# A fused linear-attention and MLP kernel: a new order for every queue, the first chunk loads ahead of the weights, and eight PSUM banks in common

## The chip, the cores and the metric

The kernel runs on one core of a Trainium2 chip. The core has a matrix engine (PE), a vector engine (DVE), a scalar engine (ACT), a general engine (POOL) and a queue engine (SP) that issues its DMAs. Each engine takes its instructions in the order in which the program lists them, and waits for others by semaphores. The metric is the device time of one execution in microseconds.

## The reference

The first half is a gated linear attention, one state per batch and head. The second is an MLP with a hard-swish between its two matrix products.

```python
batch, n_heads, seq, head_dim = (4, 8, 768, 48)
...
for t in range(S):
    state = alpha[:, :, t, :, None] * state + np.einsum('bhd,bhe->bhde', k[:, :, t], v[:, :, t])
    y[:, :, t] = np.einsum('bhd,bhde->bhe', q[:, :, t], state)
...
x = np.ascontiguousarray(attn_out.transpose(0, 2, 1, 3)).reshape(B * S, H * D)
...
n_tokens, d_model, d_ff = (3072, 384, 2048)
h = x @ w_in
relu6 = np.clip(h + 3.0, 0.0, 6.0)
g = h * relu6 / 6.0
return (g @ w_out).astype(np.float32)
```

All arithmetic of the kernel is in 32-bit floats; the two MLP weights come in as 64-bit floats and are converted on the chip.

## The kernel before

**Tiling.** A chunk is 128 tokens of one batch: 24 chunks, six to a batch. Two chunks make a group of the MLP (256 tokens, 12 groups). The state is carried from chunk to chunk, with a half chunk (64 tokens) as the inner step.

**The order is written by hand.** The body is one list of 1788 words (lines 751 to 900) that `run` (line 745) takes one after the other; each word names a step, a chunk or group, and the buffers. `tc.manual_schedule()` keeps this order on every engine. So the word list gives, at one stroke, the order of PE, DVE, ACT, POOL and of SP's DMAs. A word of one engine that waits holds up the later words of that engine only.

**Words of the attention** (first number: the chunk). `la`, `lk`, `lq` (line 248) and `lv` (267) load alpha, k, q and v on SP. The first six chunks are loaded by token into `rings` (192 KB a load) and turned on PE by `ta`, `tk`, `tq` (274, L282); later ones come in blocks and are turned on DVE (L286), by `ca` for alpha. `ca` (297) places alpha: a copy on ACT (L300) for the first six. `r` (304, L309) and `p` (316, L320) are DVE scans that make the decays; `k` and `q` (324, L332) multiply by them on DVE. `kb` and `ck` (371, 376) turn k by token on PE and ACT; from chunk 8 on `kt`, `kw`, `kr` do it over DRAM. `sc` (338, L346) makes scores on PE, `m` (349, L356) masks them on DVE, `qa` (360, L366) and `sv` (412, L419) place q and the state with ACT. `u` (422, L429) is the state's update on PE, `sm` (434, L437 and L439) adds it on DVE, `st` (407, L409) decays the state on POOL. `ya`, `yb` (448, L455) make the output on PE, `cy` (461, L464) copies it to `xT` with ACT.

**Words of the weights** (16 slices of 768 KB: 0 to 7 of the first weight, 8 to 15 of the second). `w` (155, L162 and L166) loads a slice as pairs of 32-bit words. `d1` and `d2` (183, 194) take its low and high words on ACT, `dx` (188, L191) the sign on ACT for slices 0, 1, 2 and 4. `d3` (199) builds the bits on DVE: L207, L208 and L210, or L203 and L205 for the four. `d4` (213, L217) adds the low part on POOL. Five staging buffers (`raws`) are used in turn; two of them lie in the space of a later MLP result.

**Words of the MLP.** For the first two groups `f`, or `fa` and `fb` by halves (L478, L489), are the first product, `fr` and `fg` the gate on ACT and DVE, and `b` (L516) the second product of group 0. From group 2 on the first product is a fast matrix scheme with 20 products `M` (592, L600) in place of 24: `y` (577) makes 25 sums of weight blocks and `xc` (586) 11 sums of inputs on DVE (`add`, lines 537 to 541), `n` (604, L606) keeps partial results with ACT, `o` (608) makes outputs on DVE, `e` and `h` (619, 623) are the gate. The second product is a scheme of seven products `P` (685, L703) from group 1 on, with sums `x` of weights and `s` of hidden values (649, 658, L647), results kept by `K` (ACT) or put out by `G` (L719 on DVE, L716 on ACT), and `O` stores them. `z.m.n` (529, L532) issues n idle matmuls to bank m.

The two steps that the prediction speaks of most: `y.23` makes weight block 2 on DVE (L541), and `M.2.1`, the second product of group 2, is the first that reads it. `PRODUCTS` at line 560 pairs each product with its input and weight block.

**PSUM.** The attention's words name one of four banks `t0` to `t3` (`banks`, line 223), those of the MLP and the idle matmuls one of four banks `m0` to `m3` (`bank_m`, line 470). A step that starts a new result in a bank waits until the earlier result has been read out by ACT or DVE.

Of the kernel before, what the change touches and what calls it, by code (L numbers as in the profile page):

```python
# [17 lines left out]
def kernel(  # L18
# [42 lines left out]
    G = 2  # L61
# [161 lines left out]
    banks = [ps.tile([C, NP * C], FP, tag=f"t{i}", name=f"t{i}_ps") for i in range(4)]  # L223
# [246 lines left out]
    bank_m = [ps.tile([C, GT * 2], FP, tag=f"m{i}", name=f"m{i}_ps") for i in range(4)]  # L470

# [278 lines left out]
    with tc.manual_schedule():  # L750
        run("""z.0.5 z.0.3 z.0.1 z.0.8 qa.0.0 w.0 d2.0 d3.0 la.0 ta.0.0 ca.0 r.0 lk.0 tk.0.1 k.0
               z.0.2 p.0 la.1 ta.1.2 lq.0 tq.0.3 ca.1 r.1 lk.1 lv.0.0 sv.0.0 d1.0 kb.0.0 ck.0 z.0.2
               u.0.2.1 sm.0.0 sv.0.1 q.0 qa.0.1 tk.1.0 k.1 p.1 z.0.2 sc.0.2.3 m.0 la.2 ta.2.0 ca.2
               dx.0 w.2 d2.2 kb.1.0 ck.1 lq.1 r.2 sm.0.1 st.1 tq.1.2 q.1 d3.2 z.0.3 d1.2 dx.2 lv.1.1
               u.1.3.1 sv.1.0 sm.1.0 p.2 sm.1.1 sc.1.0.2 m.1 ya.0.3 yb.0 cy.0 lq.2 w.1 d1.1 tq.2.1
               q.2 d4.2 lk.2 tk.2.3 k.2 fa.2.0 d4.0 st.2 sc.2.0.2 d2.1 d3.1 m.2 dx.1 d4.1 qa.1.1
               lk.3 la.3 ta.3.1 ca.3 la.4 fa.0.1 sv.1.1 w.3 r.3 ta.4.3 ca.4 r.4 tk.3.1 k.3 kb.2.0
               qa.1.0 d2.3 ya.1.2 yb.1 cy.1 fa.1.2 lq.3 ck.2 d1.3 p.3 d3.3 lv.2.2 u.2.3.2 sm.2.0
               d4.3 fb.2 tq.3.1 q.3 fb.1 qa.2.0 sm.2.1 sv.2.0 st.3 fr.0.2.0 fg.0.2 lk.4 tk.4.0
               sv.2.1 w.5 d2.5 k.4 d3.5 d1.5 qa.3.0 d4.5 qa.2.1 sc.3.1.3 m.3 w.6 d2.6 d1.6 d3.6 d4.6  # L760
               lv.3.0 lq.4 w.7 kb.3.2 fb.0 f.0.3.3 kb.4.0 ya.2.1 ck.3 u.3.3.2 sm.3.0 fr.0.3.1 fg.0.3
               fr.0.1.0 fg.0.1 qa.3.1 sv.3.0 sm.3.1 p.4 d2.7 sv.3.1 d1.7 d3.7 d4.7 f.0.5.0 fr.0.5.1
               fr.0.0.0 fg.0.5 fg.0.0 tq.4.3 ck.4 la.5 ta.5.2 f.0.6.3 ca.5 w.4 d2.4 ya.3.0 yb.3 cy.3
               fr.0.6.1 yb.2 cy.2 w.9 d2.9 q.4 qa.4.1 d1.4 d1.9 dx.4 la.6 w.8 d3.4 r.5 lk.5 w.10
               d3.9 p.5 ca.6 fg.0.6 d4.9 w.12 lq.5 lv.4.1 d2.8 d3.8 f.0.7.2 d1.8 st.4 d4.8 d4.4 w.11
               fr.0.7.0 fg.0.7 f.1.7.0 fr.1.7.1 fg.1.7 sc.4.0.2 m.4 f.1.1.1 fr.1.1.0 fg.1.1 f.1.3.3
               fr.1.3.1 d2.10 d1.10 tk.5.3 f.1.0.2 d2.12 d3.10 d4.10 w.13 fg.1.3 fr.1.0.0 fg.1.0 k.5
               d3.12 lq.6 f.1.6.0 f.1.2.1 u.4.1.0 sm.4.0 d1.12 d4.12 sv.4.0 qa.4.0 ya.4.2 fr.1.6.1
               fg.1.6 w.15 tq.5.3 fa.4.3 sv.4.1 d2.11 kb.5.1 d2.13 fr.1.2.0 f.1.4.2 fr.1.4.1 d1.11
               sm.4.1 q.5 r.6 d3.11 d3.13 fg.1.4 d4.11 lv.5.0 lk.6 tq.6 p.6 d2.15 d3.15 fg.1.2 d1.13  # L770
               d4.13 sc.5.0.3 yb.4 f.1.5.0 fr.1.5.1 fg.1.5 tk.6 m.5 b.1.0.2 fb.4 b.1.1 d1.15 d4.15
               st.5 y.5 w.14 la.7 lk.7 cy.4 d2.14 qa.5.1 ck.5 b.0.0.1 fr.0.4.0 d3.14 k.6 q.6 ca.7
               fg.0.4 d1.14 d4.14 x.0 y.1 y.10 b.0.1 y.0 y.2 u.5.2 P.1.0.0 K.1.0 qa.5.0 sv.5.0
               qa.6.1 P.1.1.3 b.0.2 b.1.2 kb.6.0 ya.5.3 y.6 s.1.0.0 sm.5.0 sv.5.1 G.1.0.0 tk.7
               s.1.1.1 s.1.2.3 x.1 yb.5 cy.5 b.1.3 sc.6.1.2 lv.6.2 ck.6 u.6.3.0 s.1.3.2 x.2 P.1.2
               b.0.3 K.1.1 y.7 s.1.4 s.1.5 y.11 y.3 r.7 xc.2.1 x.3 y.4 y.8 xc.2.3 k.7 xc.2.0 xc.2.4
               y.9 y.12 y.16 y.13 y.15 P.1.3.3 K.1.2 P.1.4 bo.1 P.1.5 xc.2.5 G.1.1.1 P.1.6 y.14 y.17
               y.19 xc.2.6 sm.6.0 G.1.2.2 y.20 M.2.0.2 lv.12.1 la.8 O.1.1 O.1.0 ca.8 y.18 y.21 y.23
               so.1 G.1.3.3 n.2.0.8 bo.0 lq.7 lv.7.0 O.1.2 m.6 xc.2.2 xc.2.10 xc.2.7 tq.7 r.8 p.7
               xc.2.8 sv.6.1 M.2.15.3 M.2.1 kb.7.3 n.2.1.9 M.2.16 M.2.2 n.2.2.10 M.2.7.0 n.2.7.11  # L780
               sm.6.1 xc.2.9 q.7 p.8 M.2.3 M.2.4 n.2.4.12 M.2.8 o.2.0.0 M.2.5 n.2.5.13 qa.7.0 sv.6.0
               st.7 lk.8 O.1.3 lq.8 lk.9 la.9 la.10 tk.8 tq.8 lq.10 lq.9 ya.6.1 yb.6 M.2.9 z.1.3
               M.2.18.1 o.2.1.0 e.2.1.1 M.2.10 cy.6 ck.7 sc.7.0.2 u.7.1.3 n.2.10.14 M.2.11 qa.7.1
               ca.9 la.11 y.22 M.2.6.2 h.2.1 q.8 m.7 e.2.0.0 h.2.0 n.2.11.15 qa.6.0 n.2.18.10 qa.8.1
               M.2.12 M.2.19 n.2.12.12 M.2.13 sm.7.0 sv.7.1 r.9 k.8 o.2.3.0 sv.7.0 ya.7.0 y.24
               o.2.5.0 n.2.13.12 o.2.2.0 yb.7 cy.7 sc.8.1.2 xc.3.1 o.2.2.1 e.2.2.1 xc.3.3 o.2.3.1
               M.2.14 xc.3.4 xc.3.0 xc.3.5 o.2.4.0 xc.3.7 xc.3.6 o.2.6.0 P.2.0.1 M.3.0.2 M.2.17
               h.2.2 o.2.6.1 e.2.3.0 h.2.3 o.2.7.0 K.2.0 n.3.0.12 M.3.1 n.3.1.9 e.2.5.1 M.3.7.0
               n.3.7.13 xc.3.8 o.2.7.1 xc.3.2 kt.8 e.2.6.0 h.2.6 tk.9 M.3.2 n.3.2.10 e.2.4.0 P.2.1.3
               h.2.4 h.2.5 s.2.0.14 e.2.7.0 G.2.0.1 h.2.7 M.3.3 M.3.4 n.3.4.8 k.9 s.2.1.11 M.3.8  # L790
               o.3.0.0 ca.10 kt.9 P.2.3.3 s.2.2.15 s.2.3.14 lv.8.2 kw.8 kr.8 lk.10 sm.7.1 xc.3.9
               M.3.5 n.3.5.11 K.2.2 e.3.0.1 xc.3.10 M.3.9 o.3.1.0 P.2.2 K.2.1 u.8.0.3 M.3.18.2 s.2.5
               M.3.10 n.3.10.14 n.3.18.15 e.3.1.0 s.2.4 P.2.4 tq.9 h.3.0 st.8 sv.8.0 M.3.11 n.3.11.8
               tk.10 p.9 sm.8.0 q.9 r.10 k.10 qa.9.0 qa.9.1 m.8 sm.8.1 h.3.1 M.3.19 o.3.5.0 kt.10
               P.2.5 G.2.2.0 st.9 M.3.12 sc.9.0.1 qa.8.0 n.3.12.10 o.3.3.0 kw.9 lv.9.0 kr.9 sv.8.1
               u.9.2.3 sm.9.0 sv.9.1 sv.9.0 G.2.1.2 sm.9.1 st.10 M.3.15.2 M.3.16 M.3.6.3 M.3.13 m.9
               o.3.4.0 o.3.6.0 tq.10 n.3.13.10 o.3.2.0 e.3.4.1 ya.8.2 yb.8 ya.9.3 yb.9 cy.9 M.3.14
# [135 lines left out]
```

## Time and profile before

| | |
|---|---|
| median of three runs | 535.38 us (535.36 to 535.48) |
| span of the profiled execution, first to last instruction | 533.7 us |
| PE busy | 524.6 us, 98% |
| DVE busy | 477.2 us, 89% |
| ACT busy | 257.2 us, 48% |
| POOL busy | 50.4 us, 9% |
| DMA queue of the program | 53.44 MB, 42.5% of the 16 engines' time |
| first transposes of loaded data on PE (L282) | at 8.05 us |
| last copy, on ACT (L716) | 530.86 to 531.18 us |

The profiled execution has no total of its own beside the span; the runs' median is 1.7 us above it. PE here is the matmul row; a 32-bit matmul takes several passes and shows as two instructions (58 for the 29 idle matmuls), a transpose as one. Durations of neighbouring instructions of one engine overlap a little: a DVE step of 0.68 us that follows another without a wait starts 0.60 us after it.

### The profile page before, as it was taken

What the parts mean: (1) busy time and instruction counts of PE and PEld (TensorE: products, weight loads), DVE (VectorE), ACT (ScalarE), POOL (GpSimd) and SP (SyncE); (2) the same over time, 40 slices, a digit from 0 to 9 for tenths busy, and PEclk for the clock granted to TensorE, in tenths of its full rate; (3) what the DMA queues carried; (4) which work ended last, traced back from release to release, by engine and by line L of the source; (5) the groups of instructions that cost most, each with busy time, mean ns of one, the idle gap of its engine ahead of it and who ended that gap; (6) DMA issues with size and microseconds to landing.
All of it is one profiled execution on the core that took longest, in us unless ns stands there. A gap on an engine that the chain in (4) does not pass through costs nothing.

```text
span 533.7 us, 15143 instructions
## 1 busy us (share of the span) xinstructions
PE 524.6 (98%) x6306; PEld 499.4 (94%) x6306; DVE 477.2 (89%) x849; ACT 257.2 (48%) x503; POOL 50.4 (9%) x71
## 2 busy tenths in 40 slices
PE   8799999999999999999999999999999999999997
PEld 7698886789999999999999999999999999999997
DVE  6999989999999999998999999999999899496382
ACT  3889865212653553553544444642634544553340
POOL 5333425100000000000000000000000000000000
DMA  9998876005615155254344355044454042100001
GB/s 174 217 252 256 215 216 152 21 2 154 152 30 116 32 121 135 57 140 95 87 110 113 91 124 140 19 120 102 115 136 104 11 110 43 44 2 2 15 16 37
DMA packets 124100, 54.40 MB, mean 102 GB/s; under 512 B 83328, under 2 KB 116864, under 8 KB 124032
## 3 DMA queue, kind: packets, MB, share of 16 engines
q1 hardware_dynamic: 124032, 53.44, 42.5%
q8 instruction: 49, 0.80, 0.6%
q14 instruction: 19, 0.16, 0.1%
HBM read 44.50 MB, written 8.91 MB: 100 GB/s over the span
## 4 chain that ended last, share of the span: by engine, by line
PE 85%; DVE 8%; POOL 2%; DMA 2%; ACT 1%; issue 1%; SPq 1%; DVEq 0%; POOLq 0%
PE m_ps L703 34%; PE m_ps L600 34%; PE m_ps L478 5%; PE t_ps L455 4%; PE t_ps L346 2%; PE t_ps L429 2%; PE m_ps L489 2%; PE t_ps L282 1%; DVE rings L647 1%; DMA v<-in_v_dram 1%; DVE raw L537 1%; ACT raw L191 1%; DMA kq<-in_k_dram 1%; DVE g_sb L647 1%; DVE w L537 1%
## 5 line engine op out<-in xcount | busy, mean ns | idle before, releaser
L606 ACT COPY g_sb<-m_ps 128x512 f32<-128x512 f32 x110 | 63.6, 584 | 124.9 <-PE m_ps L600 104.1
L703 PE MATMUL m_ps<-w,g_sb 128*128 128x192 f32 x704 | 121.7, 327 | 0.0
L703 PEld LDWEIGHTS m_ps<-w,g_sb 128*128 128x128 f32 x704 | 113.7, 190 | 0.4
L703 PE MATMUL m_ps<-rings,g_sb 128*128 128x192 f32 x528 | 91.5, 326 | 0.0
L703 PEld LDWEIGHTS m_ps<-rings,g_sb 128*128 128x128 f32 x528 | 85.4, 190 | 0.1
L600 PE MATMUL m_ps<-xc,w 128*128 128x128 f32 x640 | 82.7, 277 | 0.3 <-DVE w L541 0.3
L600 PEld LDWEIGHTS m_ps<-xc,w 128*128 128x128 f32 x640 | 77.5, 192 | 1.5 <-issue 0.5
L494 ACT ACTIVATE r<-g_sb,half 128x512 f32<-128x512 f32 x80 | 56.8, 722 | 32.9 <-DVE g_sb L541 12.1
L498 DVE SCALAR_TENSOR_TENSOR g_sb<-r,g_sb 128x512 f32<-128x512 f32 x80 | 53.6, 682 | 4.6 <-ACT r L494 4.2
L600 PE MATMUL m_ps<-xT,raw 128*128 128x128 f32 x400 | 52.5, 277 | 0.0
L600 PEld LDWEIGHTS m_ps<-xT,raw 128*128 128x128 f32 x400 | 48.6, 192 | 0.6
L409 POOL TENSOR_TENSOR st<-sm,R 128x192 f32<-128x192 f32 x20 | 12.9, 643 | 353.8 <-DVE sm L439 306.7
L647 DVE TENSOR_TENSOR g_sb<-g_sb 128x512 f32<-128x512 f32 (+1 forms) x55 | 42.0, 795 | 0.2
L600 PE MATMUL m_ps<-xT,w 128*128 128x128 f32 x320 | 42.0, 276 | 0.0
L600 PEld LDWEIGHTS m_ps<-xT,w 128*128 128x128 f32 x320 | 39.3, 192 | 0.1
L366 ACT COPY A<-q 48x256 f32<-48x256 f32 x88 | 35.5, 404 | 5.0 <-DVE q L332 3.7
L356 DVE TENSOR_TENSOR A<-t_ps,mask 64x256 f32<-64x256 f32 x96 | 36.0, 414 | 0.4
L478 PE MATMUL m_ps<-xT,w 128*128 128x256 f32 x144 | 32.8, 382 | 0.0
L600 PE MATMUL m_ps<-xc,raw 128*128 128x128 f32 x240 | 31.8, 276 | 0.0
L309 DVE TENSOR_TENSOR_SCAN R<-t,ones 128x516 f32<-128x516 f32 x24 | 29.7, 1236 | 1.1 <-ACT t L300 1.0
L478 PEld LDWEIGHTS m_ps<-xT,w 128*128 128x128 f32 x144 | 26.7, 190 | 3.6
L600 PEld LDWEIGHTS m_ps<-xc,raw 128*128 128x128 f32 x240 | 29.6, 192 | 0.1
(104 smaller groups left out, 731.0 us busy)
## 6 DMA issues: line engine op xcount, KB each, us to landing
raw<-in_moe_w_out_dram SPq DMA_DIRECT2D x8, 768.0 KB, 5.2
raw<-in_moe_w_in_dram SPq DMA_DIRECT2D x6, 768.0 KB, 6.8
v<-in_v_dram SPq DMA_DIRECT2D x48, 96.0 KB, 3.0
out_dram<-oh SPq DMA_DIRECT2D x44, 96.0 KB, 1.7
far<-kq SPq DMA_DIRECT2D x64, 64.0 KB, 2.2
kb<-far SPq DMA_DIRECT2D x64, 64.0 KB, 2.0
aq<-in_alpha_dram SPq DMA_DIRECT2D x36, 96.0 KB, 2.5
qq<-in_q_dram SPq DMA_DIRECT2D x36, 96.0 KB, 2.4
```

What stands on the lines that cost most here:

```text
L309: nc.vector.tensor_tensor_scan(out=reverse(R, n - 1, n), data0=reverse(ax, n, n), data1=reverse(ones, n, n), initial=0.0, op0=ALU.mult, op ...
L356: nc.vector.tensor_tensor(out=to[:, a], in0=sc[a][half], in1=mask[half, half].unsqueeze(1).to_broadcast([HB, NP, HB]), op=ALU.mult)
L366: nc.scalar.copy(out=to[:, a], in_=Q_t[j][64 * a : 64 * a + D, :, half])
L409: nc.gpsimd.tensor_tensor(out=st, in0=sm, in1=R_t[j][:, :, 0:1].to_broadcast([C, NP, D]), op=ALU.mult)
L455: nc.tensor.matmul(y_of(j, (i + 1) // 2, p)[:, HB * b : HB * b + HB], vb[:, p, e : e + 32], A_t[j][:, b, 2 * p + a], start=(b == 0 and i = ...
L478: nc.tensor.matmul(h[:, f], w1[:, kk, o : o + C], xT_t[g][:, kk], start=(kk == 0), stop=(kk == KT - 1))
L494: nc.scalar.activation(out=to, in_=h, func=AF.Relu, bias=half, scale=1.0 / 6.0)
L498: nc.vector.scalar_tensor_tensor(out=to, in0=r, scalar=1.0, in1=h, op0=ALU.min, op1=ALU.mult)
L600: nc.tensor.matmul(acc[g][i][:, f * C : (f + 1) * C], spots[w][:, f * C : (f + 1) * C], x_of(g, x), start=(first and f == 0), stop=last, s ...
L606: nc.scalar.copy(out=slots[z], in_=acc[g][i])
L647: nc.vector.tensor_tensor(out=out, in0=in0, in1=in1, op=ALU.subtract)
L703: nc.tensor.matmul(to[g], a, rhs[:, f], start=(first and f == 0), stop=(last and f == HF - 1), skip_group_check=True)
```

## The change

One line exchanges the bank lists, so that both halves of the kernel can name all eight banks (for the attention, 4 to 7 are the MLP's, and the other way round), and the whole word list is replaced. The steps are the same 1788, the same 29 idle matmuls among them; their order and their buffers differ. At the head of the list ten loads of chunks 0 to 2 and weight slice 1 now come ahead of slice 0, which was the first transfer; only five idle matmuls stand in front of the first transposes, against seventeen; and five idle steps (ten matmuls) stand in the middle of the first third. Around the first products of group 2 some attention steps of chunks 7 to 9 have moved ahead of `y.23`.

```diff
     bank_m = [ps.tile([C, GT * 2], FP, tag=f"m{i}", name=f"m{i}_ps") for i in range(4)]
+    banks, bank_m = banks + bank_m, bank_m + banks
...
-        run("""z.0.5 z.0.3 z.0.1 z.0.8 qa.0.0 w.0 d2.0 d3.0 la.0 ta.0.0 ca.0 r.0 lk.0 tk.0.1 k.0
-               z.0.2 p.0 la.1 ta.1.2 lq.0 tq.0.3 ca.1 r.1 lk.1 lv.0.0 sv.0.0 d1.0 kb.0.0 ck.0 z.0.2
-               u.0.2.1 sm.0.0 sv.0.1 q.0 qa.0.1 tk.1.0 k.1 p.1 z.0.2 sc.0.2.3 m.0 la.2 ta.2.0 ca.2
-               dx.0 w.2 d2.2 kb.1.0 ck.1 lq.1 r.2 sm.0.1 st.1 tq.1.2 q.1 d3.2 z.0.3 d1.2 dx.2 lv.1.1
...
-               d4.13 sc.5.0.3 yb.4 f.1.5.0 fr.1.5.1 fg.1.5 tk.6 m.5 b.1.0.2 fb.4 b.1.1 d1.15 d4.15
-               st.5 y.5 w.14 la.7 lk.7 cy.4 d2.14 qa.5.1 ck.5 b.0.0.1 fr.0.4.0 d3.14 k.6 q.6 ca.7
...
-               y.19 xc.2.6 sm.6.0 G.1.2.2 y.20 M.2.0.2 lv.12.1 la.8 O.1.1 O.1.0 ca.8 y.18 y.21 y.23
-               so.1 G.1.3.3 n.2.0.8 bo.0 lq.7 lv.7.0 O.1.2 m.6 xc.2.2 xc.2.10 xc.2.7 tq.7 r.8 p.7
-               xc.2.8 sv.6.1 M.2.15.3 M.2.1 kb.7.3 n.2.1.9 M.2.16 M.2.2 n.2.2.10 M.2.7.0 n.2.7.11
...
+        run("""z.2.5 la.0 ta.0.0 z.7.3 qa.0.0 ca.0 lk.0 tk.0.0 la.1 z.0.3 ta.1.6 ca.1 lq.0 lk.1 r.0
+               k.0 p.0 kb.0.4 ck.0 r.1 tq.0.7 lv.0.0 sv.0.0 tk.1.0 lq.1 k.1 u.0.1.2 q.0 qa.0.1 la.2
+               kb.1.5 sm.0.0 sm.0.1 st.1 w.1 ck.1 sv.0.1 p.1 tq.1.6 sc.0.1.0 lv.1.1 sv.1.0 lk.2 q.1
+               qa.1.0 ta.2.5 ca.2 m.0 sc.1.2.7 w.0 d1.1 m.1 d2.1 d3.1 z.0.8 dx.1 lq.2 qa.1.1
...
+               fg.0.6 lq.5 r.5 tq.5.3 q.4 w.7 p.5 w.4 kb.4.5 d1.7 lk.6 ck.4 lv.4.1 sv.4.0 w.9 d2.7
...
+               d4.8 b.1.0.4 d3.10 la.6 ca.6 w.11 fr.1.0.0 d4.3 fg.1.0 fg.1.1 d1.10 f.1.3.3 z.6.3
+               d1.11 sv.4.1 lq.6 fr.0.4.0 f.1.2.0 d4.10 d3.12 w.13 qa.4.1 z.2.1 tk.6 r.6 k.6 d1.12
...
+               z.4.2 bo.0 y.10 s.1.4 G.1.0.1 y.8 z.6.2 y.2 y.0 y.4 lq.9 y.12 y.16 q.7 xc.2.0 xc.2.7
+               s.1.5 qa.7.1 K.1.1 P.1.4 y.14 y.9 y.15 y.13 y.17 y.19 K.1.2 P.1.5 O.1.0 G.1.1.1
+               O.1.1 xc.2.8 y.20 x.3 sc.6.7.0 lk.9 kb.7.3 y.18 G.1.2.0 tq.8 qa.7.0 O.1.2 M.2.0.5
+               st.7 n.2.0.8 P.1.6 lv.7.2 y.21 y.23 la.10 M.2.1 m.6 M.2.7.1 n.2.1.15 M.2.2 xc.2.9
...
```

## The prediction

> **What bounds the kernel now.** I read the page's shares first, then the table of stretches, then the waits of PE, then the timeline at the places these point to.
>
> ```profile
> PE 524.6 (98%) x6306; PEld 499.4 (94%) x6306; DVE 477.2 (89%) x849; ACT 257.2 (48%) x503; POOL 50.4 (9%) x71
> ...
> 24.00:76.00 52.00, 51.52 (x682) 45.42 (x681) 49.66 (x82) 45.45 (x76) 21.54 (x19) 1.00 0.89 233
> 76.00:128.00 52.00, 51.75 (x438) 41.12 (x436) 51.40 (x77) 15.45 (x32) 8.89 (x14) 1.00 0.34 79
> 128.00:424.00 296.00, 295.96 (x3809) 291.04 (x3810) 284.09 (x520) 141.99 (x297) 10.12 (x15) 1.00 0.43 100
> ```
>
> The columns after the length are PE, PEld, DVE, ACT, POOL. From 128 us on PE is busy 295.96 of 296 us, and the waits of PE after 128 us are one of 0.3 us. So behind that point nothing can be gained: time is saved only by getting PE to this point earlier, or by having less PE work left there. From 76 to 128 us DVE is just as full (51.40 of 52). The place where the two meet:
>
> ```profile
> 127.20 0.69 DVE L541 SCALAR_TENSOR_TENSOR w<-w 128x512 f32<-128x512 f32 x1
> ...
> 128.04 1.13 PE L600 MATMUL m_ps<-xc,w 128*128 128x128 f32 x8 [0.29 <-DVE w L541]
> ```
>
> The first line is step `y.23`, the second is `M.2.1`, which waits for it. Hence the frame of my sum: **span = time at which DVE ends `y.23` + PE work from `M.2.1` on + tail.** Now that is 127.9, then from 128.04 to PE's end at 530.84, then 2.9 us for the last copy and store: 533.7. The runs' median is 535.38, 1.7 above the span; I carry this 1.7 unchanged.
>
> How DVE got to 127.9:
>
> ```profile
> 8.05 1.04 PE L282 MATMUL t_ps<-ident,rings 128*128 128x128 f32 x8
> ...
> 9.31 1.23 DVE L309 TENSOR_TENSOR_SCAN R<-t,ones 128x516 f32<-128x516 f32 x1 [1.02 <-ACT t L300]
> ...
> 72.56 0.36 DVE L439 TENSOR_TENSOR s<-t_ps,st 128x192 f32<-128x192 f32 x1 [1.28 <-PE t_ps L429]
> ...
> 82.47 1.78 DVE L207 TENSOR_SCALAR w<-w 128x768 f32<-128x768 f32 x1
> ...
> 92.80 1.95 DVE L332 TENSOR_TENSOR q<-q,P 128x512 f32<-128x512 f32 x1
> ```
>
> From the first scan (`r.0`, 9.31) DVE runs 118.6 us to the end of `y.23`. Its steps up to there, each at the time from its start to the next one's start (0.60 for a 128x512 of 0.68, since neighbours overlap by 0.08: the pair of L498 takes 1.28), make 110.6. The rest, 8.0, is the one wait of 1.28 at 72.56; 3.4 in four steps that stretch while POOL runs an add (L207 1.78 where it takes 0.55 elsewhere, `q.6` 1.95 where it takes 0.69, and two smaller ones at 26.1 and 29.4); and 3.2 in small pieces.
>
> **The change part by part.**
>
> *The PE list as work.* Both lists hold the same 1788 steps, the idle matmuls (29, 58 instructions) included. PE's work is the same; only places differ. From `M.2.1` to the end, counted with 0.112 us a pass of L600, 0.163 of L703 and 0.48 of a `ya` or `yb`, the old list has 398.6 us left and the new one 398.4: **-0.2**. (The actual 402.8 from 128.04 to 530.84 has 4.2 more, about 0.1 at each change of kind; no wait, so I keep it.)
>
> *The DVE list.* Every DVE step that stands before `y.23` in the old list also stands before it in the new one. Nine more do: `ca.9`, `tq.7`, `tq.8` (three L286 transposes, 0.95 each), `p.7` (1.14), `q.7` (0.66), `sm.6.1` (0.27) and three `xc` (0.20 each), taken from the same rows: 2.85 + 1.14 + 0.66 + 0.27 + 0.60 = **+5.5**. They are in front of `M.2.1` on a full engine, and `M.2.1` is in front of everything else on PE. They are not lost work (less is left for later), but later DVE has time to spare, as it idles 107 - 73 = 34 us from 424 on, so it buys nothing at the end. The same holds a little behind: before `o.2.1.0` there are 6.5 us more, so moving the meeting point does not mend it.
>
> *First loads in front of the weights.* On SP `w.0` (768 KB, ahead of all) goes behind ten chunk loads and `w.1`. ACT starts on `w.0` at 5.63, so that load took 4.9 us from its issue at 0.75; a store of 192 KB lands in 2.0 us in the table of issues. `la.0` is 192 KB and first now: between these ends, 3.5, so it lands at 4.3. The way from the first transposes to the scan (8.05 to 9.31) is 1.26; these four now run at the first matmuls' rate, 0.2 us apart instead of 0.11 (34 idle ones in 6.75 us against 4 in 0.61 later): 0.4 more. `r.0` at about 6.15, so DVE is 3.2 earlier. But `d3.0`, two instructions of 1.39 us, ran in the hole in front of `r.0` and now stands behind it on the full engine. Net **-1.8**, bounds -2.5 (the five idle matmuls that stay in front hold PE to 3.7) and -0.4 (4.9 us for the load).
>
> *Waits on the way.* The 1.28 at `sm.4.0` came from PE being late with `u.4`; in the old list PE has 59.6 us of steps up to `u.4` and DVE 60.1 ahead of `sm.4.0`, in the new one 45.6 and 47.2, so PE is more ahead there: **-1.3** (bounds -1.3 and 0). Against that `r.1` and `k.1` follow transposes on a PE that is still at the slow rate, with `z.7.3` and `z.0.3` between them, and `d3.5` comes a microsecond earlier on DVE while its `w.5` has 22 loads in front of it instead of 21: I put **+0.5** (bounds 0 and 2: the row for it is the 2.39 us for which DVE waited on `w.0`).
>
> *Row first, then a page:* the old list's 34 idle matmuls keep PE busy from 1.46, and the spacing drops from 0.213 to 0.111 us at 7 us. The Trainium skill, "TensorE: Matmul & The Clock Gate", Part 1, has the clock at half by default, released by about 3.4 us of sustained activity. The new list has 5 idle matmuls ahead of `ta.0` and then a hole; by that rule full speed could come a window later, and about 1.5 us would be added to the start, by the row alone 0.5.
>
> *POOL's adds.* 16 (L217, 1.5 to 1.9 us each) lie before `y.23` in both lists. The rows show that a DVE step which reads SBUF alone (L207, L309, `q.6`) is held when it starts under an add, while L498, L356 and L439, which read PSUM, are not. I keep **3.4** for the new list, change 0 (bounds -3.4, no step held, and +3.4, twice as many: `d4.1`, `d4.8`, `d4.13` and `d4.14` are followed by SBUF steps in the new list).
>
> *Eight shared banks.* PE's waits that can be a bank not yet drained stand before 30 us (L374 on ACT's L300 0.7, L282 on DVE's L439 0.3 and L356 0.2); no DVE step waited for PE until 72.56, so they are not on the path. What the sharing allows by itself is worth **0** (bounds -0.3, the one wait from 128 us on, and +0.5 for a bank that now waits for the slower of two uses, as those first waits of 0.2 to 0.7).
>
> *SP, ACT.* The same transfers and copies; behind 50 us the DMA engines are under half busy, ACT is at 48%. Nothing added. ACT is full only from 24 to 76 us (45.45 of 52), where conversions come later by one load; that is in the 0.5.
>
> *Sum:* +5.5 - 0.2 - 1.8 - 1.3 + 0.5 = **+2.7**: `M.2.1` at about 131, span 536.4, time 535.38 + 2.7 = 538.1.
>
> **The rivals.**
>
> 1. *POOL's adds miss DVE (the other side).* If the new list puts a PSUM-reading step under each add, the 3.4 us go; then +2.7 - 3.4 = -0.7: 534.7. From 0.7 us of stretch on (0.3 with `r.0` half a microsecond earlier as well, 534.2) the new kernel is ahead. For it: behind `d3.5`, `d3.9` and `d3.10` stand 2 us of PSUM steps. Against: behind `d3.8` comes `d3.3`, behind `d3.14` come `q.6` and the `y` steps, all from SBUF.
> 2. *Weights too late.* Eight chunk loads in front of `w.1`, and `la.5`, `lk.5`, `lq.5` in front of `w.7`: DVE waits for `d3.5`, `d3.6` or `d3.7` while the DMA engines are saturated (0.89 of their time from 24 to 76 us). At 2.2 us for one weight load a wait of one to two loads: +2.7 + 2.2 to 4.4 = 540.3 to 542.5. Against: by the order of loads only `w.5` comes within a microsecond of its use.
> 3. *It does nothing.* DVE is not the bound up to `y.23`, since PE waited only 0.29 us for it, and PE's early work, equal in both, decides. Then the earlier start and the later `d3.0` cancel to within 1 us: 534.5 to 536.4. Against: a step that is 5.5 us late on a full engine is not hidden by a slack of 0.29.
>
> **How the numbers follow.** The forecast, with its terms near the middle (536.5 to 540), has 0.54; rival 2 0.12; rival 3 0.16; rival 1 0.18, of which two thirds lie below 534.3. About 0.2% (1.07 us) is what a measurement of this kernel can tell from no change. Faster by more than that: rival 1's lower part, 0.13. Within: the rest of rival 1 and rival 3, 0.21. Slower: 0.66. All bounds on the good side add up to -2.2 (533.2), all on the bad side to +10.8 (546.2); with 2 in 10 left out, 533.8 to 541.8.
>
> **What would show it.** Right: `r.0` starts near 6.2; the DVE step before `M.2.1` ends near 131, with PE idle for microseconds between 90 and 135 us, where it now idles 0.3; PE's waits after `M.2.10` are small again; the tail is 2.9. Wrong: `r.0` after 7, the start is mis-sized; `M.2.1` before 128, then DVE's stretch, in particular under L217, was smaller; PE waits after 150 us, then DVE stayed the bound beyond the meeting point and the loss is larger; a wait of DVE for ACT at L203 or L207 between 20 and 50 us is rival 2.

## The result and the profile after

The changed kernel takes **560.66 us** (median of four runs, 557.9 to 561.81) against 535.43 for the one before: a ratio of 1.0463, 95% interval 1.0436 to 1.049. The forecast was 538.1, range 533.8 to 541.8: the sign was right, the size was wrong by 22.6 us.

The profiled execution of after has a span of 559.6 us, 26.0 more than before. The share of PE on its page, then its table of the same three stretches (length, then PE, PEld, DVE, ACT, POOL, granted clock, DMA share, GB/s):

```profile
PE 534.1 (95%) x6306; PEld 504.6 (90%) x6306; DVE 490.9 (88%) x849; ACT 257.6 (46%) x503; POOL 50.0 (9%) x71
```

```profile
24.00:76.00 52.00, 47.05 (x594) 40.79 (x592) 48.91 (x75) 38.16 (x61) 18.46 (x23) 0.97 0.97 234
76.00:128.00 52.00, 47.86 (x374) 37.42 (x374) 51.23 (x71) 20.42 (x38) 11.17 (x9) 1.00 0.38 103
128.00:424.00 296.00, 288.20 (x3695) 280.57 (x3696) 281.60 (x508) 133.98 (x280) 8.45 (x14) 0.99 0.41 94
```

PE idles 5.0, 4.1 and 7.8 us in the three stretches, where it idled 0.5, 0.3 and 0.04. DVE is as full as it was. The clock, 1.00 throughout before, is 0.97 and 0.99 in two rows: the records of after show three stretches of 3.4 us at half rate, at 25.5, 131.3 and 343.0 us.

The timeline of after at the start and at the meeting point (start, length, engine, line, operation; in brackets the idle time before it and what ended it):

```profile
5.87 1.23 DVE L309 TENSOR_TENSOR_SCAN R<-t,ones 128x516 f32<-128x516 f32 x1 [1.69 <-ACT t L300]
...
139.41 2.77 PE L704 MATMUL m_ps<-rings,g_sb 128*128 128x192 f32 x16
...
140.24 0.69 DVE L542 SCALAR_TENSOR_TENSOR w<-w 128x512 f32<-128x512 f32 x1
...
142.02 1.05 PE L601 MATMUL t_ps<-xc,w 128*128 128x128 f32 x8
```

`r.0` starts at 5.87 (before 9.31). `y.23`, the DVE line, ends at 140.9 (before 127.9). `M.2.1`, the last line, starts at 142.02 (before 128.04); it comes 1.1 behind `y.23`, because `P.1.6` in front of it was itself late, behind a PE that had stood still and then run at half rate. From `M.2.1` to PE's end at 556.80 pass 414.8 us (before 402.8), and the tail is 2.8. So the 26.0 are **14.0 ahead of `M.2.1` and 12.0 behind it**. Behind it PE waits again; the waits of PE in after from there on (line, what it waited for, us in total, times, longest):

```profile
PE t_ps L429 <- DMA kb<-far: 1.4, 2, 0.8
PE t_ps L601 <- DVE g_sb L540: 1.1, 1, 1.1
PE m_ps L429 <- DMA kb<-far: 0.9, 2, 0.7
...
PE t_ps L601 <- ACT g_sb L607: 0.5, 1, 0.5
```

They come to 5.5 us, the last of more than half a microsecond at 364; the same view of before has 0.3 in all, the wait in front of `M.2.1` itself. But the waits are only half of the 12.0. PE's stretch from `M.2.1` to its end, before and then after (length, then PE, PEld, DVE, ACT, POOL, granted clock, DMA share, GB/s):

```profile
128.04:530.82 402.78, 402.78 (x4906) 396.46 (x4906) 357.04 (x656) 182.07 (x377) 11.15 (x17) 1.00 0.35 83
```

```profile
142.02:556.80 414.78, 408.72 (x4905) 399.37 (x4904) 356.77 (x645) 180.98 (x372) 9.77 (x16) 1.00 0.32 75
```

After's PE stands still for 6.1 us of it; for the other 5.9 it is shown busy longer with the same work. The half-rate stretch at 343.0 makes at most 1.7 of these; what the remaining 4.2 are, no view names. The chain of waits of after also goes through DVE far behind the meeting point. This is its order of time (start, length, engine and line):

```profile
183.78 1.02 DVE R L309
...
184.93 0.66 DVE k L332
185.59 0.61 DVE g_sb L538
...
186.24 1.17 PE t_ps L601 x8
...
187.44 0.69 DVE g_sb L542
188.13 0.62 DVE kq L391
```

A scan and a scaling of a later chunk's attention (L309, L332) stand ahead of a sum of the MLP (L538) for which PE waits, here 0.28 us; then the chain is on DVE again. What PE waits for is not an input: the sum reads out the bank that PE's next product writes. A late DVE holds PE in this way too, by a bank that is not yet free.

**Theory A**, formed on this: in the new list PE and DVE stay level up to about 365 us, so whatever holds DVE is paid, also behind `M.2.1`; in the old list DVE runs ahead from 128 us on. **Theory B**: the 12.0 belong to the new rest's own order, banks or transfers. **Theory C**: all of it comes from the head.

### The profile page after: what moved, and what is told of

Read it like the earlier page. It is cut to its first block, busy times and chain, and to the rows that moved or that the text cites. A ratio compares the mean times of both kernels' runs of the same rounds, so it can differ in the third digit from the quotient of the medians.

```text
span 559.6 us, 15091 instructions
## 1 busy us (share of the span) xinstructions
PE 534.1 (95%) x6306; PEld 504.6 (90%) x6306; DVE 490.9 (88%) x849; ACT 257.6 (46%) x503; POOL 50.0 (9%) x71
## 4 chain that ended last, share of the span: by engine, by line
PE 49%; DVE 33%; issue 5%; DMA 4%; ACT 4%; SPq 4%; POOL 1%; DVEq 0%; POOLq 0%; ACTq 0%
PE m_ps L704 16%; PE t_ps L601 15%; PE m_ps L601 6%; PE t_ps L704 6%; DVE g_sb L499 3%; DVE g_sb L538 3%; DVE R L309 3%; DMA aq<-in_alpha_dram 2%; DVE P L320 2%; DVE g_sb L648 2%; DVE k L286 1%; DVE A L356 1%; DVE q L286 1%; DVE k L332 1%; SPq L404 1%
## 5 line engine op out<-in xcount | busy, mean ns | idle before, releaser
L607 ACT COPY g_sb<-t_ps 128x512 f32<-128x512 f32 x74 | 43.0, 584 | 89.7 <-PE t_ps L601 81.1
L704 PE MATMUL m_ps<-w,g_sb 128*128 128x192 f32 x432 | 75.4, 327 | 1.3 <-DVE g_sb L665 1.3
L704 PEld LDWEIGHTS m_ps<-w,g_sb 128*128 128x128 f32 x432 | 70.3, 191 | 2.6 <-DVE g_sb L665 1.6
L601 PE MATMUL t_ps<-xc,w 128*128 128x128 f32 x384 | 51.3, 278 | 2.7 <-DVE g_sb L540 1.1
L601 PEld LDWEIGHTS t_ps<-xc,w 128*128 128x128 f32 x384 | 47.1, 191 | 4.2 <-DVE g_sb L540 1.3
L704 PE MATMUL t_ps<-w,g_sb 128*128 128x192 f32 x272 | 47.2, 327 | 0.0
L704 PEld LDWEIGHTS t_ps<-w,g_sb 128*128 128x128 f32 x272 | 43.9, 190 | 0.1
L607 ACT COPY g_sb<-m_ps 128x512 f32<-128x512 f32 x36 | 20.9, 584 | 35.6 <-PE m_ps L601 28.1
L538 DVE TENSOR_TENSOR g_sb<-g_sb 128x512 f32<-128x512 f32 x40 | 27.0, 684 | 10.8 <-ACT g_sb L607 10.4
L601 PE MATMUL m_ps<-xc,w 128*128 128x128 f32 x256 | 33.7, 276 | 0.0
L309 DVE TENSOR_TENSOR_SCAN R<-t,ones 128x516 f32<-128x516 f32 x24 | 30.9, 1286 | 1.8 <-ACT t L300 1.7
L601 PEld LDWEIGHTS m_ps<-xc,w 128*128 128x128 f32 x256 | 31.2, 192 | 0.2
```

The source lines that it names most:

```text
L309: nc.vector.tensor_tensor_scan(out=reverse(R, n - 1, n), data0=reverse(ax, n, n), data1=reverse(ones, n, n), initial=0.0, op0=ALU.mult, op ...
L538: eng.tensor_tensor(out=out, in0=in0, in1=in1, op=ALU.add if s1 > 0 else ALU.subtract)
L601: nc.tensor.matmul(acc[g][i][:, f * C : (f + 1) * C], spots[w][:, f * C : (f + 1) * C], x_of(g, x), start=(first and f == 0), stop=last, s ...
L607: nc.scalar.copy(out=slots[z], in_=acc[g][i])
L704: nc.tensor.matmul(to[g], a, rhs[:, f], start=(first and f == 0), stop=(last and f == HF - 1), skip_group_check=True)
```

## The experiments

All times beside 535.4 to 535.7 us for the kernel before on the same chip. "Rest" is PE's time from `M.2.1` to its end. The median is of all executions of a run; `y.23`, `M.2.1`, rest and span are of the one that was profiled, and executions of one kernel with the new list or a part of it differ by 2 to 4.4 us. Kernels with "small adds" or "short h" leave out part of the arithmetic.

| run | median us | ratio, 95% interval | `y.23` ends | `M.2.1` | rest | span |
|---|---|---|---|---|---|---|
| before | 535.4 | | 127.9 | 128.0 | 402.8 | 533.7 |
| after | 560.7 | 1.0463 (1.0436 to 1.049) | 140.9 | 142.0 | 414.8 | 559.6 |
| e1, old head, new rest | 559.9 | 1.0459 (1.0426 to 1.0492) | 127.8 | 128.0 | 425.7 | 556.4 |
| e7, the same, loads mended | 558.7 | 1.0430 (1.0415 to 1.0445) | 127.7 | 127.9 | 425.1 | 555.8 |
| e2, new head, old rest | 550.7 | 1.0278 (1.0258 to 1.0298) | 140.5 | 142.6 | 403.0 | 549.6 |
| e3, new, small adds | 552.3 | 1.0314 (1.0289 to 1.0339) | 133.6 | 133.8 | 412.5 | 549.1 |
| e4, old, small adds | 534.8 | 0.9988 (0.9979 to 0.9998) | 127.2 | 127.3 | 402.8 | 533.0 |
| e5, new, short h | 553.0 | 1.0330 (1.0315 to 1.0345) | 142.8 | 142.9 | 407.2 | 553.0 |
| e6, old, short h | 535.4 | 0.9997 (0.9988 to 1.0006) | 127.9 | 128.0 | 402.8 | 533.6 |
| e9, new, both | 548.1 | 1.0230 (1.0215 to 1.0246) | 135.3 | 135.4 | 406.4 | 544.7 |
| e10, new, nine behind | 560.5 | 1.0465 (1.0449 to 1.0481) | 135.6 | 136.2 | 420.6 | 559.6 |
| e8, old, loads first | 535.1 | 0.9999 (0.9986 to 1.0012) | 127.1 | 127.2 | 402.8 | 532.9 |
| e11, old, faster start | 536.9 | 1.0024 (1.0013 to 1.0035) | 131.8 | 132.0 | 402.8 | 537.6 |
| e12, old, warm start | 534.7 | 0.9982 (0.9974 to 0.9991) | 127.2 | 127.3 | 402.8 | 532.9 |
| e13, new, idle matmuls | 574.6 | 1.0712 (1.0694 to 1.0730) | 155.0 | 156.5 | 414.4 | 573.7 |

### Halves of the two lists

One list is cut at `M.2.1`, and what is left follows in the order of the other; all with the line that exchanges the bank lists.

```diff
 e1   words of the old list up to M.2.1, then the words not yet done in the new list's order
 e2   words of the new list up to M.2.1, then the words not yet done in the old list's order
 e7   e1 with:
+     lk.8 lq.8 la.9 ahead of y.12, lk.9 ahead of P.1.5, la.10 ahead of y.18
```

> The new order up to M.2.1, then all that is left in the old order. Theory A: DVE has done nine steps more by M.2.1 than the old rest asks for, so PE no longer waits behind it: M.2.1 at 142, then 402.8 and 2.9, span 547.7 (546 to 549.5), PE waits after 145 us under 1 us in all. Theory B': the 12.0 us come from what the head left behind (clock, banks, DMA): 559. Theory C: the head is all of it and worth 25: also 559.

Theory A. `M.2.1` is as late as with the whole new list, and then there is no loss. PE from 176 us on (length, PE, PEld, DVE, and so on):

```profile
176.00:424.00 248.00, 248.00 (x3186) 244.09 (x3185) 237.85 (x436) 114.81 (x240) 8.62 (x13) 1.00 0.44 102
```

248.00 of 248.00 us busy. The 12.0 us go with the order of the rest. This is no test of the sharing of banks: the old order keeps its bank numbers, and behind `M.2.1` none of its 131 steps that name a bank names one of the other half, while 80 of 131 do in the new order. So the new rest's banks go together with its order here, and no run takes them apart. The span is 1.9 over the 547.7 of theory A: 0.6 in `M.2.1`, 1.1 in the tail of 4.0, 0.2 in the rest.

> The old order up to M.2.1, then all that is left in the new order, on eight shared banks. Theory A (the new order has PE and DVE level for 340 us, so that every hold of DVE counts, also behind M.2.1): M.2.1 starts at 128 as before, but DVE still has the nine steps (5.5 us) to do ahead of what PE needs next, PE waits for DVE some 10 to 15 us in all between 128 and 370, and as DVE comes out of the head 7.5 us less late than with the new head (23.4 against 15.9 us beyond its steps at y.23), the span is 7.5 under the new order's 559.6: 552 (549 to 554). Theory B (the 12.0 us behind M.2.1 belong to the new rest itself, banks or order, whatever stands ahead): 128.0 + 414.8 + 2.9 = 546. Theory C (all comes from the head): 534.

None of the three numbers. The old head brings PE to `M.2.1` at 128.0, and 10.9 us more than with the new head are lost behind it. Part of that is the seam's own. The first of DVE's waits in e1:

```profile
DVE k L286 <- DMA kq<-in_k_dram: 6.7, 2, 4.1
```

The new list has chunk loads in its head that the hybrid only issues behind the cut. Hence e7.

> As the first hybrid (old order up to M.2.1, new order for what is left), but with the loads lk.8, lq.8, la.9, lk.9 and la.10 earlier in the old head, so that DVE no longer waits 6.7 us for them behind the seam. Theory A: M.2.1 at 128 to 129; DVE, whose work up to 365 us is that of the new order and which comes 7.5 us less late out of the head, keeps PE waiting: rest 419 to 424, span 550 to 555. Theory B (the new rest costs 12.0 by itself): rest 414.8, span 546. Theory C (the new rest costs nothing when the head is old): 534.

The DMA wait for k is gone (one of 2.2 us for q is left) and the span is 555.8, above A's range by 0.8 and 10 above B: an old head does not help a new rest, which refutes C. But the seam is still not clean. The longest wait of PE in e7:

```profile
PE m_ps L601 <- ACT g_sb L607: 8.4, 1, 8.4
```

The ACT copy is queued behind the copies of `qa.7`, which wait for `q.7` on DVE, and 10.2 us at half rate follow. Without these 8.4 the rest of 425.1 would by this estimate be 416.7, close to B's 414.8. So e1 and e7 don't decide between A and B; the next runs do.

### Taking load off DVE

```diff
 e3, e4, e9   add_low (L217, POOL)
+        dst, high, lo = (x[:, :, 0:8] for x in (dst, high, lo))
 e5, e6, e9   hidden1 (step h, L499)
-        times(gs[0][:, 4 * n : 4 * n + 4, i * C : (i + 1) * C], v(r), v(h))
+        times(gs[0][:, 4 * n : 4 * n + 2, i * C : (i + 1) * C], v(r)[:, 0:2], v(h)[:, 0:2])
```

> The new kernel with POOL's add of the weights (L217) on 8 columns of each row instead of 256 or 384, so the rest of the weights lacks its low word; everything else is as before. Theory A with POOL's adds as the largest mis-sized term: DVE's steps L203, L207, L208, L309, L332, L542 are no longer held, y.23 ends 6 to 8 us earlier (133 to 135), and since DVE is the bound up to 340 us the span falls by as much: 551 to 553. If the hold of DVE is not by POOL's adds: L208 keeps its mean of 904 ns and the span stays within 2 us of 559.6.

> The old kernel with the same small adds on POOL. DVE loses 3.4 us of holds before y.23, but PE waited only 0.3 us there and 0.6 us in all after 30 us, so theory A gives a gain of 0.3 to 1 us: span 532.7 to 533.4, M.2.1 at 127 to 127.8 without a wait. If DVE alone set M.2.1 (the frame of the prediction): 3.4 us earlier, span 530.3.

Both as theory A has them, except that the new kernel gains more: `y.23` 7.3 and `M.2.1` 8.2 us earlier, the median 8.3, the span 10.5 (the profiled execution is the fastest of four in e3 and the second slowest of four in after; 549.1 is 1.9 under the expected range). The old one gains 0.6 (0.7 in the span) from losing 3.4 us of holds. The same edit is worth more than ten times as much in the new list, where the holds themselves are not quite three times as long (9.4 against 3.4, below). Where it sits, from the timeline of after, POOL's adds and the DVE steps that start under them:

```profile
59.13 1.95 POOL L217 TENSOR_TENSOR w<-w,g_sb 128x768 int32<-128x768 int32 x1 [0.95 <-DVE w L205]
```

```profile
59.40 2.10 DVE L208 TENSOR_SCALAR w<-w 128x768 uint32<-128x768 uint32 x1
```

The add ends at 61.08. L208 starts 0.27 us into it and ends 0.42 after it, 2.10 us instead of 0.56. So do others: `r.2` takes 2.65, `k.6` 1.68, `d3.3`'s and `d3.14`'s L208 1.61 and 1.70, `y.5` 1.95. Over what these and the smaller ones take elsewhere, the stretches ahead of `y.23` come to 9.4 us; before it was 3.4. The group L208 of after and then of e3 (line, shapes, count, busy us, mean ns, idle before):

```profile
L208 DVE TENSOR_SCALAR w<-w 128x768 uint32<-128x768 uint32 x12 | 10.9, 904 | 0.4
```

```profile
L208 DVE TENSOR_SCALAR w<-w 128x768 uint32<-128x768 uint32 x12 | 7.3, 608 | 0.4
```

Before it was 605 ns: the old order met the adds with other steps.

> The new kernel with every product of the gate (step h, L499, 80 of them, all behind M.2.1) on half its columns, so half of the hidden layer stays stale. That takes about 0.27 us of DVE each, 21.6 in all, 12 of them before 365 us; PE's work and M.2.1 stay as they are (142). Theory A (PE waits behind M.2.1 because DVE is level with it): PE's time from M.2.1 on falls from 414.8 to 403 to 407, span 548 to 552. Theory B (the shared banks, DMA or PE's own order make these 12 us): 413 to 415, span 558 to 560.

> The old kernel with the same halved step h (L498). PE waits for nothing behind M.2.1 there, so theory A and B both say no change: 402.8 us from M.2.1 on, span 533.7; at most 0.5 less.

Theory A on both. Nothing of PE's work, banks or transfers is changed, and 7.5 of the 12.0 us behind `M.2.1` go (up to 1.7 of them with the half-rate stretch at 343.0, which e5 has not); in the old list the same 21.6 us of DVE are worth nothing. What is left behind `M.2.1` in e5 is 4.4 us over the old rest. PE's waits there, the fourth of them in front of `M.2.1` itself:

```profile
PE m_ps L429 <- DMA kb<-far: 0.9, 2, 0.6
PE t_ps L429 <- DMA kb<-far: 0.7, 1, 0.7
PE t_ps L601 <- issue: 0.5, 2, 0.3
PE t_ps L601 <- DVE w L542: 0.4, 1, 0.4
PE t_ps L601 <- DVE g_sb L540: 0.2, 1, 0.2
```

Without that one they come to 2.3 us, 1.6 of them for the keys read back from HBM (`kb<-far`); for the remaining 2.1 PE is shown busy longer than before, and no view says why. Whether the shared banks have a part in the 4.4 no run tells. The span is 1.0 above the expected 552, as `M.2.1` came 0.9 later; 13.7 us at half rate lie ahead of it in that run (6.8, 3.4 and 3.4), against 6.8 in after. It is the slowest of four executions; the other three have spans of 550.9 to 551.3, inside the range.

> The new kernel with both reliefs of DVE, POOL's small adds and the halved step h (the weights lack their low word, half of the hidden layer stays stale). Theory A (holds by POOL's adds in the head, a level DVE behind M.2.1): the two gains add up, M.2.1 at 134 and 403 to 406 from there on, span 540 to 543; what is left over the old 533.7 is the nine steps (5.5) and one to four microseconds of other waits. If a further cause were in the banks or in PE's order, the span would stay above 545.

The rest is 406.4, 0.4 above its range; `M.2.1` is at 135.4, not 134, and the span 1.7 above the range. It is the fastest of four executions; the other three have spans of 546.1 to 547.3, above the 545 that were to point to a further cause. So one is not excluded. PE waited 3.0 us for DVE at 70 us (L480 in that file, `f.1.2.0`) and then ran 6.8 us at half rate. By the medians the two reliefs bring 12.5 us together and 8.3 and 7.7 singly: they do not quite add up.

### The nine steps

```diff
 e10, on the new list
-     tq.7 xc.2.10 sm.6.1 p.7 ca.9 q.7 xc.2.7 xc.2.8 tq.8 at their places ahead of y.23
+     the same behind M.2.1, each ahead of the step that needs it (qa.7, st.7, la.11 and lq.9 with them)
```

> The new kernel with the nine DVE steps that it has ahead of y.23 and the old one has not (5.5 us) moved behind M.2.1, each in front of the step that needs it. The prediction's frame (DVE up to y.23, then PE without a wait): y.23 and M.2.1 5 us earlier and the span with them, 553.5 to 555. Theory A (DVE stays the bound up to 340 us and has the same work to do by then): M.2.1 4 to 6 us earlier, but PE waits as much more behind it, span 558 to 560.

Theory A. `y.23` ends 5.3 earlier and `M.2.1` starts 5.8 earlier, the rest is 5.8 longer, the span is 559.6 as without the move (the medians are 560.5 and 560.7; the executions of either kernel lie 2 to 4 us apart, so the closer match of the spans is luck). Where the wait went, from PE's timeline of e10:

```profile
136.19 1.05 PE L601 MATMUL t_ps<-xc,w 128*128 128x128 f32 x8
...
148.01 1.22 PE L601 MATMUL t_ps<-xT,raw 128*128 128x128 f32 x4 [3.40 <-DVE s L439]
```

`M.2.1` is early, and 12 us later PE waits for DVE again (L439 is a state sum, behind the moved steps on DVE; it reads out the attention's bank that this product of the MLP takes next).

### The early loads alone, and a version that beats both

```diff
 e8, old list
-     z.0.5 z.0.3 z.0.1 z.0.8 qa.0.0 w.0 d2.0 d3.0 la.0 ta.0.0 ca.0 r.0 lk.0 tk.0.1 k.0 z.0.2 p.0 la.1 ...
+     la.0 lk.0 la.1 lq.0 z.0.5 z.0.3 z.0.1 qa.0.0 w.0 ta.0.0 ca.0 z.0.8 r.0 tk.0.1 k.0 z.0.2 p.0 d2.0 d3.0 ...
 e11, old list from u.0 on, behind
+     la.0 lk.0 la.1 lq.0 z.0.5 qa.0.0 w.0 ta.0.0 ca.0 z.0.3 tk.0.1 r.0 k.0 ta.1.2 p.0 d2.0 tq.0.3 ca.1 r.1
+     d3.0 lk.1 lv.0.0 sv.0.0 d1.0 kb.0.0 ck.0 z.0.2
 e12, old list from sc.0 on, behind
+     la.0 lk.0 la.1 lq.0 w.0 lv.0.0 lk.1 z.0.5 z.0.3 qa.0.0 ta.0.0 ca.0 z.0.3 tk.0.1 r.0 k.0 ta.1.2 ca.1
+     z.0.5 tq.0.3 kb.0.0 ck.0 r.1 p.0 sv.0.0 d2.0 z.0.6 q.0 d1.0 d3.0 u.0.2.1 sm.0.0 sv.0.1 qa.0.1 z.0.3
+     tk.1.0 k.1 p.1 z.0.2
```

> The old kernel with la.0, lk.0, la.1 and lq.0 in front of w.0 and d2.0, d3.0 behind p.0; nothing else moves. r.0 starts at 5.9 to 6.5 instead of 9.3 (with the new kernel 5.87). The prediction's term for this part was -1.8 (-2.5 to -0.4). Theory A: PE and DVE are both level up to 128 us, so the gain needs both to start earlier: -0.4 to -1.8. Rival: PE's idle matmuls and weights set PE's stream, and the later w.0 costs as much: -0.3 to +1.

`r.0` starts at 7.06, later than expected: nine idle matmuls still stand in front. From 14 us on every PE step is 0.7 to 0.8 us earlier; what is gained at 14 us is there at the end. The span falls by 0.8, the median by 0.3, and the interval of the ratio takes in 1. By the profiled execution the part is worth 0.8 in the old list, not 1.8; by the times it can't be told from nothing.

> The old order from u.0 on, with a head in which la.0, lk.0, la.1 and lq.0 stand in front of w.0, d3.0 behind r.1 and 12 fewer idle matmuls of the first chain (z.0.1, z.0.8 and one z.0.2 left out). The run with the loads first alone carried its 0.72 us of 14 us unchanged to the end. Theory: r.0 at 5.9 to 6.2, the streams of both engines 1.5 to 2.5 us earlier from 14 us on, span 531.2 to 532.2, time 533 to 534 against 535.4. Rival: with fewer idle matmuls TensorE stays at half rate for a window longer, and 1 to 2 us are lost again: 534.5 to 536.

The rival, and more: the time is longer, 1.0024 (535.87 to 539.41 us). The profiled execution is the slowest of twelve, 2.5 us over the median: `r.0` at 5.78, yet `M.2.1` 3.9 us *later* than before. Two stretches at half rate, 3.4 us from 13.3 and 6.8 from 23.6. The stretch of 24 to 31 us, and PE's step in it:

```profile
24.00:31.00 7.00, 6.25 (x92) 5.85 (x92) 3.47 (x7) 4.76 (x7) 4.42 (x4) 0.54 1.05 207
```

```profile
24.75 1.29 PE L455 MATMUL t_ps<-A,v 128*32 128x64 f32 x40 [2.17 <-issue]
```

The clock is 0.54 and PE is busy 6.25 of 7 us at that rate; DVE, which was busy 6.88 of these 7 us before, has 3.47. The second stretch begins in a pause of PE of 2.2 us in the middle of the attention's output (L455) for which the profile names no releaser; whether the other executions had it I can't tell. By the starts of the same DVE steps this execution is still 0.2 us ahead of before from 14 to 24 us and 3.5 behind it from 40 us on, so its loss lies in the pause and the second stretch, not in the one at 13.3. Nor is half rate the whole of the loss: one execution has a mean clock of 1.000 and takes 536.37 us, against 535.53 for before. What the eleven idle matmuls that e11 lacks have to do with it stays open.

> The old order from sc.0 on, with a head in which la.0, lk.0, la.1 and lq.0 stand in front of w.0 and lv.0 in front of lk.1, the second scan does not wait behind w.0 on ACT, and four idle matmuls more than in the old list fill PE's holes instead of twelve fewer. If the loss of the faster start was the half clock: r.0 at 5.9, no half-rate stretch behind 10 us, both streams 1 to 2 us ahead from 14 us on, span 531.7 to 532.7, time 533.4 to 534.4. If the early transposes themselves do not carry: 535 to 537.

No stretch at half rate in the profiled execution, and 534.71 us: **faster than both kernels**, by 1.0 us or 0.18% against the one before (0.9974 to 0.9991). `r.0` came at 6.75, not 5.9, and the time is 0.3 above the expected range. `m.0` is 1.2 us earlier, `M.2.1` only 0.7: what e12 gains over e8 at the very start it loses again by 128 us.

### Idle matmuls against half rate

```diff
 e13, new list
+     z.0.18 ahead of P.1.4, z.0.14 sc.5, z.0.12 f.1.2, z.0.10 f.1.6 and b.0.3, z.0.8 yb.5 and P.1.5,
+     z.0.6 sc.2 and u.16, z.0.5 tk.3 and u.17
```

> The new kernel with 102 idle matmuls more (0.11 us each, 11.4 us if none lay in a hole) ahead of eleven steps for which PE waited 0.4 to 3 us. If the half-rate stretches (three of 3.4 us in the profiled run, each at most 1.7 us of PE's time) are a cost of their own: they go or fall to one, and the time falls by 2 to 5 us, 555.5 to 558.5. If PE had time to spare wherever it was at half rate, since DVE is the bound: within 1 us of 560.7. If the idle matmuls stand in PE's way: 562 or more.

They stand in PE's way: 13.9 us slower. My price was half of the true one: each idle matmul is two passes, so the 102 are 22.6 us of PE at 0.111, and most of that came on top, 14.5 of it ahead of `M.2.1`. Half rate became rarer (one 6.8 us stretch; two of five executions have a mean clock of 0.997 and 0.999) and the rest stayed at 414.4 without any behind `M.2.1`. So half rate is not what makes the rest long. What it costs by itself in the new kernel the run does not settle: at most half of 10.2 us.

## Why the prediction was wrong

**The step that failed** is the frame: *"span = time at which DVE ends `y.23` + PE work from `M.2.1` on + tail"*, and with it *"later DVE has time to spare"*. I summed both lists up to `M.2.1` and `o.2.1.0`, and took from the old profile that PE would not wait behind it. PE did wait, and its time from `M.2.1` on grew by 12.0 where the sum had -0.2. The rest of the miss lies ahead: `M.2.1` came at 142.0 and not at about 131, because the holds by POOL's adds (9.4 us, forecast 3.4) and the waits and pieces on the way (+5.0, forecast +0.5) were mis-sized, and because `P.1.6` was late on PE (1.1 behind `y.23`). Together 12.2 and 11.0 are the 23.2 us between the forecast span of 536.4 and the measured one. The same sum, with the same durations, for steps further on (DVE's listed work up to the input + PE's listed work from the step on):

| PE step, its input | old list | new list | DVE's part, old and new |
|---|---|---|---|
| `M.2.1`, `y.23` | 510.6 | 515.9 | 112.0, 117.5 |
| `P.2.1`, `h.2.3` | 509.5 | 516.4 | 138.1, 148.3 |
| `M.4.10`, `o.4.1.0` | 507.8 | 514.3 | 190.8, 203.7 |
| `M.6.9`, `o.6.0.0` | 504.1 | 514.5 | 263.6, 277.1 |
| `M.8.9`, `o.8.0.0` | 500.2 | 510.5 | 339.8, 352.5 |

In the old list the sums fall by 10 us from `M.2.1` to `M.8.9`, in the new one by 1.4 up to `M.6.9`. The DVE steps that the new list moves forward, most of them the attention's, are 5.5 us at `M.2.1`, but 13.5 at `M.6.9`. DVE also ends each step later than its list says, by waits, holds and small pieces: at `o.6.0.0` 22.9 us in before, 33.7 in after. Of before's 22.9, 7.0 came up behind 128 us, 4.9 of them in DVE's waits for PE and ACT; in after it is 10.3 behind `y.23`, without a single wait of DVE over 0.35 us before 342 us, while PE waits for DVE. At `M.6.9` in after: 277.1 + 33.7 + 0.3 until PE starts + 245.8 to PE's end = 556.9 against the measured 556.8; in before 263.6 + 22.9 + 1.8 + 242.5 = 530.8. These two add up by construction, as the 33.7 and the 22.9 are taken from the measured ends. That PE's rest depends on DVE's load in the new list, and not in the old one, is shown by e2 (old rest: no loss), e5 and e6 (relief behind `M.2.1`: 7.5 us in one list, none in the other) and e10 (the nine steps moved: no gain).

By its own steps:

- *What bounds before.* Half right. Behind 128 us PE alone counts (e6: 21.6 us less of DVE, no change). But up to there DVE alone does not set `M.2.1`: with 3.4 us of holds gone it came 0.7 earlier (e4), where the frame has 3.4. PE's own stream is level with DVE's there.
- *The DVE list, +5.5.* Right as a count (e10: 5.3 at `y.23`), wrong as a price: it is not this place that is paid.
- *First loads, -1.8.* `r.0` was forecast for 6.15 (its terms, 4.3 + 1.26 + 0.4, add up to 5.96) and came at 5.87, but a microsecond early at the start is not one at 128 us. Alone, in the old list, the part is worth 0.3 by the medians and 0.8 by the span (e8); e12, which moves more than the loads, has 1.0. The 1.5 us by the page's rule did not come: in the records of after PE has its full rate from 5.0 us on.
- *The wait at `sm.4.0`, -1.3, and the waits on the way, +0.5.* The former is gone, as forecast; but DVE waits at `q.3` (0.84) and elsewhere instead, 1.8 us in all behind `r.0`, and the small pieces are more; no run takes these apart. Waits and pieces up to `y.23` (without the first 6 us, the holds and that one wait) are 3.1 us in before and 8.1 in after: +5.0 where I had +0.5. DVE's wait for ACT at L203, which was my reason for the bound, is 0.4 in all. PE at half rate was no part of the sum beyond the first transposes: up to 1.7 us for each of the three stretches.
- *POOL's adds, 0 with bounds of 3.4 either way.* Mis-sized: the stretches are 9.4 instead of 3.4, +6.0 and beyond the bound, for which I had taken twice the number of held steps; without the adds `y.23` ends 7.3 earlier (e3). My reading that a step is held when it reads SBUF alone is too wide: `tq.7` (L286) starts at 96.08, 0.39 us into an add of 1.79, and takes 1.13, as elsewhere. With these sizes the head's 13.0 at `y.23` are +5.5 - 2.1 (the rounded difference of DVE's lateness at `r.0`, 8.0 in before and 6.0 in after) - 1.3 + 5.0 + 6.0; the +5.0 is what is left of its lateness when the rest is taken off, so the sum closes by itself.
- *Eight shared banks, 0.* Not shown either way: no run has the new order on separate banks. PE waits in the new rest for banks that DVE or ACT has not read out (L540 and L607 in the waits above), so what is paid there may depend on the choice of banks too.
- *PE's work from `M.2.1` on, -0.2.* As work right, as time wrong: +12.0. The text had named the sign of it: PE waits after 150 us mean that DVE stayed the bound.
- *Tail 2.9.* 2.8.
- *Rivals.* 1 came out the other way round. 2 did not happen (DVE's one wait on weights ahead of `y.23` is 0.4; its price of 2.2 us a load is in no row; before's profile page has 5.2 to 6.8 us from issue to landing). 3 is refuted; but its doubt, whether DVE alone sets `M.2.1` before, was half right, since e4 gives 0.7 and not 3.4.

Not settled: the 4.4 us left behind `M.2.1` in e5, the part of the shared banks in the 12.0, the small pieces in front of `y.23`, and the cost of half rate by itself.

## What to carry to other kernels

Where two engines are level, compare two orders not at the one place where they meet now but at every later hand-over: work of the one ahead of it plus work of the other behind it. An order whose sums stay flat has no reserve, and holds that the old order absorbs are paid: the small adds were worth 0.6 us in the one list and 8.3 in the other. And before idle instructions are taken out, look at the granted clock: they may be what holds it.

## What the runs showed that I had not expected

**TensorE's rate falls after a partly idle stretch.** In ten profiled runs the granted clock fell from 1.0 to 0.5 sixteen times, always for 3.41 us or two or three times that, on one grid of 3.41 us. In the piece of the grid ahead of each fall PE's matmuls were busy for 8% to 60% of the time. No piece with 61% or more was followed by one at half rate; between 47% and 60% both occurred. The Trainium skill, "TensorE: Matmul & The Clock Gate", Part 1, gives a free-running window of 3413 ns and has the clock go back to half after at least one idle window; the length agrees, but here a window did not have to be idle. A PE wait at 128 us in after was enough: 2.36 us, ended by ACT, in front of the fall at 131.3.

```profile
130.33 4.54 PE L704 MATMUL m_ps<-rings,g_sb 128*128 128x192 f32 x16 [2.36 <-ACT u L683]
```

**The times of the new list spread more, and the mean clock does not rank them.** The four runs of after, 561.41, 557.9, 561.81 and 559.92 us, have mean clocks of 0.991, 0.994, 0.991 and 0.996: the fastest has not the highest. Those of before lie within 0.4 us in the first four and from 534.92 to 536.82 in later rounds, with clocks of 0.996 to 1.0 and the slowest at 1.0. So half rate alone does not make the spread; what else does stays open.

**PE can pause with no releaser.** In e11 for 2.2 us and in e13 for 3.4 us, both times in the attention's products (L455), the profile gives "issue" as the reason. In both traces one transfer of 16 KB on the queue that the profile page lists as "q8 instruction" meets the pause: it runs from 21.76 to 23.24 us, the pause from 22.58 to 24.75, in e11, and from 47.94 to 49.37 inside a pause from 47.34 to 50.75 in e13. So PE may have waited for its instructions. But before has such a transfer from 22.64 to 24.08 and no pause there, so the cause is not shown.
